# Block-sparse attention with a feed-forward layer: tying the first steps of the query and key preparations to the code's order

## The chip, the cores and the metric

The kernel runs on one core of a Trainium2 chip. The metric is the device time of one launch in microseconds (us). Two runs of the kernel before took 949.08 and 949.32 us, a median of 949.2 us.

The engines are named as the profile names them: PE multiplies matrices (PEld is its weight load), DVE and ACT work on vectors, POOL is a further vector engine, and SP issues the DMAs. In this kernel every DMA is issued by SP, in the order of its one instruction stream.

## The reference

For each of 4 batches and 8 heads there are 768 queries and 768 keys of 64 values, all in single precision. Attention is block-sparse with blocks of 32 tokens: a block of queries sees its own block and the two beside it, the first and the last block, and three sampled blocks (`sampled_blocks`, drawn with the inputs). The first and the last block of queries see all keys. Scores are divided by 8, masked, put through a softmax and multiplied with the values. The heads of a token are then laid side by side to 512 numbers, and a feed-forward layer follows:

```
h = x @ w_in                  # 3072 x 512 times 512 x 2048
g = maximum(0.01 * h, h)
out = g @ w_out               # 3072 x 2048 times 2048 x 512
```

## The kernel before, in words

**Precision.** Every operand of a matrix product is split into two half-precision parts, a high one and a low one, after a scaling by a power of two. To find that power of two for a piece of queries or keys, the kernel squares the piece and sums it.

**Tiling.** The work is cut into 192 units, one per batch, tile of 64 queries (two blocks) and pair of heads. Four tiles of queries are an *item*, so there are 12 items (three per batch, `b` and `j`). The outer loop (L1027) goes over the 192 units and is called a *step* each time. In one step it emits, in the order of the letters in `CFG["ord"]` (L45), pieces of many units in flight: scores on PE (`scores`, L629), mask and minimum on DVE (`unit_ttr`, L658), exponential on ACT (`unit_exp`, L669), the high part on ACT (`unit_high`, L684), the low part on DVE and a transposing DMA of the split probabilities `pp` into `pt` (`unit_split`, L689 and L692), the product with the values on PE (`pair_av`, L714), and pieces of the feed-forward layer of an earlier item (`ffn_h` L749, L756 to L766, `ffn_o` L779, `ffn_out` L797).

**Preparing queries.** `prep_q` (L518) makes one *half*: 128 queries of all heads, enough for two tiles, so 8 steps. There are 24 halves. Its chain is: the load of `rq` (L473, issued by `load_q`; there is one buffer of it), the square with its row sums on ACT (L523, the *first operation*), a product with a matrix of ones on PE that adds up the 128 partitions (L126, called from `scale_sum`, the *sum*), four small operations on DVE (L140 to L149), the high part on ACT (L530), the low part on DVE (L532), a transposing DMA (L535, `qs`) and two DMAs that swap the halves of the partitions (L537 and L538, `qxs`). The scores need `qs` and `qxs`. The function is a generator: `side_step` (L857), the letter "p" near the end of a step, advances such generators by a quota of work.

**Preparing keys.** `prep_k` (L485) does the same for a pair of heads with a square at L494, the sum at L126, L506, L508 and a transposing DMA at L512. There are 16 of them, 4 per batch. From the second batch on they share one buffer `k16`, and two buffers `rk` take the loads.

**What sets the order.** The code emits instructions in the order above, but this isn't the order in which they run. The framework's scheduler goes over the whole program with a priority for each instruction (its place in the code, mostly) and a model of how long each takes, and puts on each engine's stream whatever is ready first by that model. On the chip each engine then runs its stream in that fixed order, and an instruction whose input hasn't come holds up all behind it. An operation that reads only a loaded buffer, as the squares do, can so come to stand far ahead of its place in the code. Groups of matmuls that are emitted through `together` (L164) stay together.

Of the kernel before, what the change touches and what calls it, by code (L numbers as in the profile page):

```python
# [13 lines left out]
F32 = mybir.dt.float32  # L14
# [5 lines left out]
P = 128  # L20
# [9 lines left out]
CFG = {  # L30
    "ahead": 3,
    "av_lag": 3,
    "bs": 1500,
    "early": 2,
    "flag": 1,
    "g": 2,
    "g_at": 0,
    "ht": 1,
    "k_at": 6,
    "k_at0": 26,  # L40
# [10 lines left out]
    "rk": 2,  # L51
    "rmax": 1.0,
    "rmin": 0.0,
    "side": 1.2,
    "side0": 1.6,
    "spair": 1,
# [9 lines left out]
def tile_block_sparse_attention_ffn(  # L66
# [19 lines left out]
    nc = tc.nc  # L86
# [20 lines left out]
    pa = ctx.enter_context(tc.tile_pool(name="pa", bufs=2))  # L107
    pf = ctx.enter_context(tc.tile_pool(name="pf", bufs=2))
    dr = ctx.enter_context(tc.tile_pool(name="dr", bufs=2, space=bass.MemoryType.DRAM))
    ps_s = ctx.enter_context(tc.tile_pool(name="ps_s", bufs=2, space=bass.MemoryType.PSUM))  # L110
    ps_o = ctx.enter_context(tc.tile_pool(name="ps_o", bufs=2, space=bass.MemoryType.PSUM))
    ps_1 = ctx.enter_context(tc.tile_pool(name="ps_1", bufs=1, space=bass.MemoryType.PSUM))

# [1 line left out]
    nc.vector.memset(zero, 0.0)  # L115

    def bank(name, tag="h"):
        return ps_1.tile([P, 512], F32, tag=tag, name=name, bufs={"h": 3, "av": 1}[tag])


    ones = cst.tile([P, P], F32, name="ones")
# [2 lines left out]
    def scale_sum(ss, n, name):  # L124
        pb = bank(f"{name}_sum")
        nc.tensor.matmul(pb[:, :n], ones, ss, start=True, stop=True)  # L126
        return pb

    def scale_of(pb, n, name, total=False, keep=None, fl="q"):

        pool, tg = (sm, "sc") if keep is None else (cst, keep)
        m = 1 if total else n
        tot = sm.tile([P, 4], F32, tag=f"tot{fl}", name=f"{name}_tot")
        if total:
            nc.vector.tensor_reduce(out=tot[:, :1], in_=pb[:, :n], op=ALU.add, axis=AX.X)
            nc.vector.tensor_scalar(out=tot[:, :1], in0=tot[:, :1], scalar1=TINY, scalar2=None, op0=ALU.max)
        else:
            nc.vector.tensor_scalar(out=tot[:, :m], in0=pb[:, :m], scalar1=TINY, scalar2=None, op0=ALU.max)  # L140
        ex = sm.tile([P, 4], I32, tag=f"ex{fl}", name=f"{name}_ex")
        nc.vector.tensor_scalar(
            out=ex[:, :m], in0=tot[:, :m].bitcast(I32), scalar1=24, scalar2=23,
            op0=ALU.logical_shift_right, op1=ALU.logical_shift_left,
        )
        inv = pool.tile([P, 4], F32, tag=f"{tg}_i", name=f"{name}_inv")
        s = pool.tile([P, 4], F32, tag=f"{tg}_s", name=f"{name}_s")
        nc.vector.tensor_scalar(out=inv[:, :m], in0=ex[:, :m].bitcast(F32), scalar1=2.0 ** 50, scalar2=None, op0=ALU.mult)
        nc.vector.reciprocal(out=s[:, :m], in_=inv[:, :m])  # L149
        return inv, s  # L150
# [3 lines left out]
    def scales(ss, n, name, **how):  # L154
        now = tc.cur_priority
        tc.cur_priority = now - CFG["bs"]
        begin = len(nc.cur_bb.bb.instructions)
        pb = scale_sum(ss, n, name)
        loose.update(i.name for i in nc.cur_bb.bb.instructions[begin:])
        r = scale_of(pb, n, name, **how)  # L160
        tc.cur_priority = now + 8
        return r

    def together(emits):  # L164

        now = tc.cur_priority
        begin = len(nc.cur_bb.bb.instructions)
        for n, emit in enumerate(emits):
            if n == 1:
                tc.cur_priority = now - 100000  # L170
            emit()
        new = nc.cur_bb.bb.instructions[begin:]
        for i in new[1:]:
            tc.add_manual_dep(i, new[0].name, mybir.DependencyInfo(
                mybir.DependencyClass.NoSync, mybir.DependencyReason.DATA), reason="together")
        tc.cur_priority = now + len(new)
# [308 lines left out]
    def prep_k(b, hp, rk):  # L485

        nm = f"k{b}_{hp}"
        ss = sm.tile([P, 1], F32, tag="ssk", name=f"ss_{nm}")
        if b == 0:
            k16 = early_k.bitcast(F16)[:, (NP + hp) * 2 * S:(NP + hp + 1) * 2 * S].rearrange(  # L490
                "p (n l d) -> p n l d", n=HC, l=2)
        else:
            k16 = pa.tile([P, HC, 2, D], F16, tag="k16", name=f"k16_{nm}", bufs=1)
        nc.scalar.activation(flat(k16)[:, :S], flat(rk), AF.Square, accum_out=ss)  # L494
        yield 1.0
        yield 0.01
        pb = scale_sum(ss, 1, nm)
        yield 0.2
        inv, s = scale_of(pb, 1, nm, fl="k")
        if (b, "inv") not in kready:  # L500
            kready[b, "inv"] = cst.tile([P, NP], F32, name=f"kinv_{b}")
        nc.vector.tensor_scalar(
            out=kready[b, "inv"][:, hp:hp + 1], in0=inv[:, :1], scalar1=-SCALE, scalar2=None, op0=ALU.mult)
        yield 0.4
        raw = rk.rearrange("p h c d -> p (h c) d")
        nc.scalar.activation(k16[:, :, 1, :], raw, AF.Copy, scale=s[:, :1])  # L506
        yield 1.0
        nc.vector.scalar_tensor_tensor(  # L508
            out=k16[:, :, 0, :], in0=raw, scalar=s[:, :1], in1=k16[:, :, 1, :], op0=ALU.mult, op1=ALU.subtract)
        if b not in kts:  # L510
            kts[b] = pa.tile([P, H, S], F16, tag="kt", name=f"kt_{b}", bufs=2)
        nc.sync.dma_start_transpose(  # L512
            out=kts[b][:, 2 * hp:2 * hp + 2, :].rearrange("p h (c t) -> p (h c) t", t=P),
            in_=k16.rearrange("p n l d -> p (n l d)"))
        kready[b, hp] = True
        yield 1.2

    def prep_q(b, j, i, rq):  # L518

        nm = f"q{b}_{j}_{i}"  # L520
        ss = sm.tile([P, 1], F32, tag="ssq", name=f"ss_{nm}")
        qa = pa.tile([P, H, 2, D], F16, tag="qa", name=f"qa_{nm}", bufs=1)
        nc.scalar.activation(flat(qa)[:, :H * D], rq.rearrange("p h d -> p (h d)"), AF.Square, accum_out=ss)  # L523
        yield 0.7
        yield 0.01
        pb = scale_sum(ss, 1, nm)
        yield 0.2
        inv, s = scale_of(pb, 1, nm)
        yield 0.4
        nc.scalar.activation(qa[:, :, 1, :], rq, AF.Copy, scale=s[:, :1])  # L530
        yield 0.7
        nc.vector.scalar_tensor_tensor(  # L532
            out=qa[:, :, 0, :], in0=rq, scalar=s[:, :1], in1=qa[:, :, 1, :], op0=ALU.mult, op1=ALU.subtract)
        qs = pa.tile([P, H, P], F16, tag="qs", name=f"qs_{nm}", bufs=2)
        nc.sync.dma_start_transpose(out=qs, in_=flat(qa))  # L535
        qxs = pa.tile([P, H, P], F16, tag="qxs", name=f"qxs_{nm}", bufs=2)
        nc.sync.dma_start(out=qxs[:D], in_=qs[D:])  # L537
        nc.sync.dma_start(out=qxs[D:], in_=qs[:D])  # L538
        qstack[b, j, i] = (qs, qxs, inv)
        yield 0.8  # L540
# [157 lines left out]
    def pair_av(pr):  # L698

        if pr.hp == 0:  # L700
            avs[pr.item.n, pr.T] = bank(f"av_{pr.nm}", "av").rearrange("p (n l t) -> p n l t", n=NP, l=2)
        pr.av = avs[pr.item.n, pr.T]
        for u in pr.units:
            require_v(u.b, u.hp, u.T)
        emits = []
        for u in pr.units[::-1]:
            n = NCH * u.parts
            for c in range(n):
                for l in range(2):
                    for hh in range(2):  # L710
                        vt = vgs[u.b, u.T][:, c, 2 * u.hp + hh, :] if u.T else v16s[u.b, u.hp][:, c, hh, :]
                        emits.append(lambda o=pr.av[hh * D:(hh + 1) * D, u.hp], a=vt[:, l * D:(l + 1) * D],
                                     m=u.pt[c // NCH][:, :, c % NCH, hh * D:(hh + 1) * D], c=c, l=l, n=n:
                                     nc.tensor.matmul(o, a, m, start=(c == 0 and l == 0), stop=(c == n - 1 and l == 1)))  # L714
        together(emits)

    def tile_evac(pr):

# [93 lines left out]
    for b in range(B):  # L812
        for j in range(NI):
# [3 lines left out]
            for k_ in range(TPI):  # L817
                for hp in range(0, NP, 2):
                    pr = Unit()
# [30 lines left out]
    def require_v(b, hp, T):  # L850
        until(("v", b), lambda: (b, hp) in v16s if T == 0 else (b, "ready") in scr)
        while T and (b, T) not in vgs:
            start_gather_v()
# [76 lines left out]
    def start_q(n):  # L930
        if n < len(halves):
            start(("q", *halves[n]), prep_q(*halves[n], rq[n]))
# [8 lines left out]
    def start_k(b, hp):  # L941
        start(("k", b, hp), prep_k(b, hp, rk[b, hp]))
# [84 lines left out]
    for u in units:  # L1027
        it, ui = u.item, u.k * NP + u.hp
        b, nb = it.b, it.b + 1
# [161 lines left out]
```

## Time and profile before

| what | number |
|---|---|
| median of two runs | 949.2 us |
| the profiled execution, whole | 946.47 us |
| its span, first to last instruction | 944.7 us |
| PE busy | 754.8 us, 80% |
| DVE busy | 609.1 us, 64% |
| ACT busy | 488.1 us, 52% |
| POOL busy | 331.3 us, 35% |
| DMA queue, share of 16 engines | 68.5% |
| mean granted clock of PE | 0.931 |

The profile is one execution. Its span is 1.8 us shorter than its own time, and its time is 2.7 us under the median of the two runs. A row such as "L523 ACT ACTIVATE" is a group of instructions of line 523 on ACT. In a row of waits the engine on the left sat idle until what stands on the right was done; the three numbers are the total in us, how often, and the longest. SP's instructions aren't counted as busy time, so SP has no share in the table; its rows are marked "SPq" and are seen in the timeline and in the chain of waits.

### The profile page before, as it was taken

What the parts mean: (1) busy time and instruction counts of PE and PEld (TensorE: products, weight loads), DVE (VectorE), ACT (ScalarE), POOL (GpSimd) and SP (SyncE); (2) the same over time, 40 slices, a digit from 0 to 9 for tenths busy, and PEclk for the clock granted to TensorE, in tenths of its full rate; (3) what the DMA queues carried; (4) which work ended last, traced back from release to release, by engine and by line L of the source; (5) the groups of instructions that cost most, each with busy time, mean ns of one, the idle gap of its engine ahead of it and who ended that gap; (6) DMA issues with size and microseconds to landing.
All of it is one profiled execution on the core that took longest, in us unless ns stands there. A gap on an engine that the chain in (4) does not pass through costs nothing. (4 is left out here: it accounts for less than half of the span.)

```text
span 944.7 us, 21784 instructions
## 1 busy us (share of the span) xinstructions
PE 754.8 (80%) x7020; PEld 492.8 (52%) x7020; DVE 609.1 (64%) x1643; ACT 488.1 (52%) x1063; POOL 331.3 (35%) x469
## 2 busy tenths in 40 slices
PE   1325456788978979979897968989888988989998
PEld 1214334465645645646554635556455655656674
DVE  4989899996857667557565565567466655745221
ACT  4565768575535456456455554456355554535121
POOL 0234665542215344243324242333323433532221
PEclk9998557799989989999999998999999999989999
DMA  9996798678685767766675978676785665555200
GB/s 209 283 276 162 162 244 187 164 148 167 141 180 128 160 121 157 160 137 130 151 165 111 171 134 147 151 146 127 151 161 125 137 136 139 120 113 123 32 23 23
DMA packets 336624, 139.38 MB, mean 148 GB/s; under 512 B 299389, under 2 KB 311678, under 8 KB 336510
## 3 DMA queue, kind: packets, MB, share of 16 engines
q1 hardware_dynamic: 336510, 137.99, 68.5%
q8 instruction: 55, 0.90, 0.4%
q14 instruction: 59, 0.48, 0.2%
HBM read 65.57 MB, written 12.58 MB: 83 GB/s over the span
## 5 line engine op out<-in xcount | busy, mean ns | idle before, releaser
L779 PE MATMUL o<-W,g 128*128 128x512 f16 x1152 | 279.1, 388 | 7.6 <-ACT ob L797 2.9
L749 PE MATMUL h<-x,W 128*128 128x256 f16 x2304 | 280.9, 279 | 0.3 <-DVE ht L760 0.3
L749 PEld LDWEIGHTS <-W 128*128 128x128 f16 x2304 | 227.2, 101 | 50.7 <-issue 10.5
L766 POOL TENSOR_TENSOR g<-ht,g 128x512 f16<-128x512 f32 x96 | 115.3, 1201 | 336.5 <-DVE g L765 201.2
L689 DVE SCALAR_TENSOR_TENSOR pp<-p,r,pp 128x384 f16<-128x384 f32 x208 | 142.5, 702 | 106.0 <-ACT pp L684 104.4
L779 PEld LDWEIGHTS <-g 128*128 128x128 f16 x1152 | 108.8, 100 | 137.4 <-issue 23.9
L669 ACT ACTIVATE p<-p,mx 128x384 f32<-128x384 f32 x208 | 125.8, 606 | 96.3 <-DVE mx L658 67.0
L591 POOL COPY kg<-kt 128x256 f16 x264 | 129.3, 510 | 131.6 <-PE s L651 74.9
L684 ACT ACTIVATE pp<-p,r 128x384 f16<-128x384 f32 x208 | 119.6, 607 | 103.9 <-DMA pt<-pp 72.0
L714 PE MATMUL av<-pt,vg 128*64 128x128 f16 x2112 | 83.0, 231 | 50.5 <-DMA pt<-pp 40.3
L658 DVE CUSTOM_DVE_ANT_0 p<-s,em,nsc 128x384 f32<-128x384 f32 x176 | 101.9, 609 | 21.1 <-PE s L651 20.0
L714 PEld LDWEIGHTS <-vg 128*64 128x64 f16 x2112 | 72.1, 116 | 77.0 <-issue 57.4
L760 DVE SCALAR_TENSOR_TENSOR ht<-h,gd,ht 128x512 f32<-128x512 f32 x80 | 59.8, 747 | 56.0 <-ACT ht L756 55.7
L756 ACT ACTIVATE ht<-h,gs 128x512 f32<-128x512 f32 x80 | 54.0, 675 | 63.9 <-PE h L749 48.7
L651 PE MATMUL s<-kg,qs_q 128*64 128x384 f16 x352 | 65.1, 364 | 12.1 <-DVE mx L658 7.7
L732 POOL TENSOR_TENSOR x<-xf,x 128x256 f16<-128x256 f32 x48 | 35.8, 745 | 90.7 <-ACT x L730 90.0
L651 PE MATMUL s<-kg,qxs_q 128*64 128x384 f16 x352 | 63.9, 357 | 4.3 <-DMA qxs_q<-qs_q 4.3
L651 PEld LDWEIGHTS <-qs_q 128*64 128x64 f16 x416 | 27.9, 116 | 68.7 <-issue 45.4
L523 ACT ACTIVATE qa_q<-rq 128x512 f16<-128x512 f32 x25 | 15.7, 628 | 68.9 <-DMA rq<-in_q_dram 68.9
L765 DVE CAST g<-ht 128x512 f16<-128x512 f32 x96 | 43.4, 452 | 8.9 <-PE o L779 7.5
L677 DVE TENSOR_SCALAR sum<-sum 128x2 f32<-128x2 f32 x96 | 24.9, 259 | 37.1 <-ACT p L669 36.1
L669 ACT ACTIVATION_READ_ACCUMULATOR p<-p,mx 128x1 f32 x208 | 38.9, 187 | 0.0
(126 smaller groups left out, 726.0 us busy)
## 6 DMA issues: line engine op xcount, KB each, us to landing
vg<-scr SPq DMA_DIRECT2D x280, 64.0 KB, 1.9
vg<-scr SPq DMA_DIRECT2D x44, 256.0 KB, 3.1
v<-in_v_dram SPq DMA_DIRECT2D x32, 192.0 KB, 3.4
qxs_q<-qs_q SPq DMA_DIRECT2D x48, 128.0 KB, 3.0
scr<-v SPq DMA_DIRECT2D x16, 384.0 KB, 3.7
W<-in_moe_w_in_dram SPq DMA_DIRECT2D x5, 1024.0 KB, 5.9
rq<-in_q_dram SPq DMA_DIRECT2D x20, 256.0 KB, 3.5
out_dram<-ob SPq DMA_DIRECT2D x20, 256.0 KB, 2.3
```

The costliest lines, as they stand in the source:

```text
L591: nc.gpsimd.tensor_copy(out=kg[:, :, slot * BLOCK:(slot + 1) * BLOCK], in_=kt[:, :, bass.ds(off, BLOCK)])
L651: nc.tensor.matmul(o, a, k, start=(n == 0), stop=(n == 1)))
L658: nc.vector.tensor_tensor_reduce(out=u.p[i], in0=u.sp[i], in1=kgs[u.b, u.T][1] if u.T else zero.to_broadcast([P, KEYS]), scale=u.nsc, scal ...
L669: nc.scalar.activation(u.p[i], u.p[i], AF.Exp, scale=-1.0, bias=u.mx[:, :1], accum_out=u.pair.sum[:, u.pi, i:i + 1])
L684: nc.scalar.activation(pp[:, 0, :], p, AF.Copy, scale=u.r)
L689: nc.vector.scalar_tensor_tensor(out=pp[:, 1, :], in0=p, scalar=u.r, in1=pp[:, 0, :], op0=ALU.mult, op1=ALU.subtract)
L714: nc.tensor.matmul(o, a, m, start=(c == 0 and l == 0), stop=(c == n - 1 and l == 1)))
L749: nc.tensor.matmul(c.ph[:, i], w, x, start=(d == 0 and m == 0), stop=(d == NP - 1 and m == 2)))
L756: nc.scalar.activation(c.t, c.ph, AF.Copy, scale=scale[1])
L760: nc.vector.scalar_tensor_tensor(out=c.t, in0=c.ph, scalar=scale[0], in1=c.t, op0=ALU.mult, op1=ALU.max)
L766: nc.gpsimd.tensor_tensor(out=c.g[:, 1], in0=c.t, in1=c.g[:, 0], op=ALU.subtract)
L779: nc.tensor.matmul(o, a, w, start=(c.first and i == 0 and m == 0), stop=(c.last and i == 1 and m == 2)))
```

## The change

A new function `hold` finds, in the code's order, the last instruction emitted before a given one on the same engine, and ties the given one behind it. The tie is an order for the scheduler, without a semaphore; no instruction is added to the stream. It is applied to the first operation (ACT) and to the sum (PE) of each preparation of queries and of keys, except in the first item of the first batch for queries and in the whole first batch for keys: 22 preparations of queries and 12 of keys. The diff also names two numbers of buffers through a setting "s" with the value 2, which leaves them at 2 and 3 as before, and adds a tie for the products with the values that the setting "hold" with its value "kq" leaves off.

```diff
+    "hold": "kq",
+    "s": 2,
...
-    ps_s = ctx.enter_context(tc.tile_pool(name="ps_s", bufs=2, space=bass.MemoryType.PSUM))
+    ps_s = ctx.enter_context(tc.tile_pool(name="ps_s", bufs=CFG["s"], space=bass.MemoryType.PSUM))
...
-        return ps_1.tile([P, 512], F32, tag=tag, name=name, bufs={"h": 3, "av": 1}[tag])
+        return ps_1.tile([P, 512], F32, tag=tag, name=name, bufs={"h": 5 - CFG["s"], "av": 1}[tag])
...
+    def hold(begin):
+
+        ins = nc.cur_bb.bb.instructions
+        prev = next((i for i in reversed(ins[:begin]) if i.engine == ins[begin].engine), None)
+        if prev is not None:
+            tc.add_manual_dep(ins[begin], prev.name, mybir.DependencyInfo(
+                mybir.DependencyClass.NoSync, mybir.DependencyReason.DATA), reason="hold")
+
+    count = lambda: len(nc.cur_bb.bb.instructions)
...
+        begin = count()
         nc.scalar.activation(flat(k16)[:, :S], flat(rk), AF.Square, accum_out=ss)
+        if b and "k" in CFG["hold"]:
+            hold(begin)
         yield 1.0
         yield 0.01
+        begin = count()
         pb = scale_sum(ss, 1, nm)
+        if b and "k" in CFG["hold"]:
+            hold(begin)
...
+        later = (b or j) and "q" in CFG["hold"]
+        begin = count()
         nc.scalar.activation(flat(qa)[:, :H * D], rq.rearrange("p h d -> p (h d)"), AF.Square, accum_out=ss)
+        if later:
+            hold(begin)
         yield 0.7
         yield 0.01
+        begin = count()
         pb = scale_sum(ss, 1, nm)
+        if later:
+            hold(begin)
...
+        begin = count()
         together(emits)
+        if pr.item.n and "a" in CFG["hold"]:
+            hold(begin)
```

## The prediction

> **What bounds the kernel now.** I began with the page, to see whether one engine fills the span.
>
> ```profile
> span 944.7 us, 21784 instructions
> PE 754.8 (80%) x7020; PEld 492.8 (52%) x7020; DVE 609.1 (64%) x1643; ACT 488.1 (52%) x1063; POOL 331.3 (35%) x469
> PE 22%; DMA 5%; SPq 2%; DVE 1%; ACT 1%; issue 1%; ACTq 0%
> PE o L779 9%; PE h L749 9%; DMA pt<-pp 3%; PE av L714 2%; PE s L651 2%; DMA qs_q<-qa_q 1%; DMA rq<-in_q_dram 1%; SPq L619 1%; SPq L621 1%; DVE p L658 0%; DVE pp L689 0%; ACT p L669 0%; ACT pp L684 0%; DMA qxs_q<-qs_q 0%; DVE ht L760 0%
> ```
>
> PE is the busiest engine, and it still idles for 944.7 - 754.8 = 190 us. ACT is busy for half of the span. The share of a whole span says little, so the second view was the busy time by stage. Its columns give the stretch, its length, the five engines, the granted clock, the DMA share and GB/s.
>
> ```profile
> 0.00:250.00 250.00, 142.48 (x1291) 95.19 (x1293) 211.51 (x560) 155.02 (x302) 100.75 (x115) 0.84 0.87 196
> 250.00:850.00 600.00, 521.44 (x5009) 337.95 (x5004) 369.90 (x1025) 308.48 (x714) 209.59 (x335) 0.96 0.69 143
> 850.00:945.00 95.00, 90.87 (x729) 59.66 (x727) 27.74 (x59) 24.56 (x47) 20.96 (x20) 0.99 0.23 50
> ```
>
> There are three stages. Up to 250 us the weights are split, and DVE leads with 211.5 of 250 us. From 250 to 850 us attention and feed-forward run together: PE has 600 - 521.4 = 78.6 us of idle time there, and ACT and DVE have far more. After 850 us PE runs almost alone. What the change can win lies mostly in the 78.6 us.
>
> Third, the waits of the engines that the change touches, ACT's rows first.
>
> ```profile
> ACT pp L684 <- DMA pt<-pp: 72.0, 33, 6.8
> ACT qa_q L523 <- DMA rq<-in_q_dram: 68.9, 20, 6.3
> ACT k_k L494 <- DMA kt<-k_k: 26.0, 7, 8.5
> ...
> PE av L714 <- DMA pt<-pp: 54.7, 29, 5.3
> PE k_sum L126 <- ACT k_k L494: 20.8, 7, 4.9
> PE s L651 <- DMA qs_q<-qa_q: 12.5, 4, 9.6
> PE q_sum L126 <- ACT qa_q L523: 2.9, 2, 2.7
> ```
>
> The square of the queries (L523) holds ACT idle for 68.9 us in 20 waits for its load, 3.4 us each. This is what the change takes hold of. But PE waits for the sums of queries only 2.9 us. Its largest wait is for `pt`, the transposed probabilities, and ACT's largest wait is for the same DMA: there are six buffers `pp`, and ACT gets none until SP has sent an old one off. An engine that waits for its output to be carried away is ahead of its carrier. So the fourth view was the carrier: SP's timeline, and the chain of waits through one of PE's longer pauses.
>
> ```profile
> 489.05 0.52 SPq L611 DMA_DIRECT2D vg<-scr  x1
> 489.62 1.54 SPq L616 DMA_DIRECT2D vg<-scr  x2
> 491.27 1.21 SPq L692 DMA_TRANSPOSE pt<-pp  x1
> 492.58 1.25 SPq L535 DMA_TRANSPOSE qs_q<-qa_q  x1
> 493.89 0.57 SPq L473 DMA_DIRECT2D rq<-in_q_dram  x1
> 494.56 1.29 SPq L692 DMA_TRANSPOSE pt<-pp  x1
> ```
>
> ```profile
> 756.96 1.22 SPq L692
> ...
> 765.84 0.06 issue
> 765.95 2.78 DMA pt<-pp
> 768.77 0.94 PE av L714 x24
> ```
>
> ```profile
> SPq L808 <- ACT ob L797: 60.7, 4, 40.4
> SPq L692 <- DVE pp L689: 13.3, 13, 1.4
> ```
>
> SP's rows follow one another with about 0.1 us between them. Before PE's pause that ends at 768.77 us the chain runs through SP instructions for 9 us without a wait. The only large wait of SP, 60.7 us, is for the outputs in the tail. So up to its last transposition SP issues without a stop, and its stream is the bound of attention. The Trainium skill has this case in "Perfetto Trace Analysis", section "What DMA-bound means": the issuing engine's track is solid with DMA slices. By that rule a wait on ACT that goes away leaves the time at 949. The trace agrees, by the rows just shown.
>
> The fifth view is the tail: SP's last transpositions, PE's last product with values, and PE's last work.
>
> ```profile
> 874.94 4.63 SPq L692 DMA_TRANSPOSE pt<-pp  x3
> 895.63 0.86 PE L714 MATMUL av<-pt,vg 128*64 128x128 f16 x24
> 934.66 6.21 PE L779 MATMUL o<-W,g 128*128 128x512 f16 x28
> ```
>
> SP ends at 874.94 + 4.63 = 879.6 us. With 2.8 us for landing (the row above) the last product could start at 882.4; it starts at 895.6, as PE is still busy with older feed-forward work. What follows it, about 45 us, is the last item's feed-forward part, which needs all of its tiles. So PE's backlog is worth at most 895.6 - 882.4 = 13 us as long as SP ends where it does.
>
> **The change part by part.** No instruction is added: the ties are orders within one engine. What moves is seen best in one preparation (ACT, PE and DVE rows; SP's are above at 492.58 and 493.89).
>
> ```profile
> 465.41 0.63 ACT L523 ACTIVATE qa_q<-rq 128x512 f16<-128x512 f32 x1 [6.25 <-DMA rq<-in_q_dram]
> ...
> 470.77 0.67 ACT L756 ACTIVATE ht<-h,gs 128x512 f32<-128x512 f32 x1
> ...
> 484.61 0.38 PE L126 MATMUL q_sum<-ss_q,ones 128*128 128x1 f32 x2
> ...
> 488.67 0.75 DVE L532 SCALAR_TENSOR_TENSOR qa_q<-rq,q_s,qa_q 128x512 f16<-128x512 f32 x1
> ```
>
> *The squares of queries* (22 held). ACT waits 6.25 us for a load here, then squares. In the code's order the square stands behind the activation `ht` at 470.77, so it would start at 471.44, 6.0 us later, and the wait is gone. The sum runs only at 484.61, nearly 19 us after the square, so nothing behind it moves: not the low part at 488.67, not the transposition that SP reaches at 492.58, 3.2 us after that has ended (489.42), nor the two swaps and the next load of `rq`, which needs its one buffer back from L532. For the square alone the price is zero, covered by those 19 us.
>
> What does ACT's idle time give when it goes? The upper bound is 68.9 us; the lower one is 0, as ACT then waits for `pp` buffers instead. Between them, the page's chain puts about 1% of the span, some 9 us, on the load `rq`, and the next late thing in that chain is SP. I take less than half of it, 4 us, because a pause of PE that ends with an SP transfer only grows by what an earlier pause loses.
>
> *The squares of keys* (12 held). Their 26.0 us on ACT are waits for `kt<-k_k`, the single buffer `k16` being carried away by SP, not for loads. Put beside the code's order, most of these squares run behind their neighbour already, so the tie does nothing, and both this wait and PE's 20.8 us on their sums stay. Bounds: 0 to 20.8 us; I take 0.
>
> *The sums.* In the preparation above the sum already follows its preceding group in the code, so its tie does nothing. It does where the sum had jumped ahead:
>
> ```profile
> 291.13 0.63 ACT L523 ACTIVATE qa_q<-rq 128x512 f16<-128x512 f32 x1 [4.59 <-DMA rq<-in_q_dram]
> 298.70 0.38 PE L126 MATMUL q_sum<-ss_q,ones 128*128 128x1 f32 x2
> 308.24 1.17 DVE L532 SCALAR_TENSOR_TENSOR qa_q<-rq,q_s,qa_q 128x512 f16<-128x512 f32 x1
> 309.98 0.61 ACT L669 ACTIVATE p<-p,mx 128x384 f32<-128x384 f32 x1 [1.87 <-DVE mx L658]
> 317.03 1.67 SPq L535 DMA_TRANSPOSE qs_q<-qa_q  x1
> 321.59 0.60 SPq L538 DMA_DIRECT2D qxs_q<-qs_q  x1
> 331.15 0.35 PE L651 MATMUL s<-kg,qs_q 128*64 128x384 f16 x2 [0.57 <-DVE mx L658]
> ```
>
> Here the code places the square behind the activation at 309.98, so it starts at 310.6 and ends with its read-out near 311.4. The sum follows at 311.4 instead of 298.7, 12.7 us later, and the low part ends at 308.24 + 1.17 + 12.7 = 322.1. SP stands ready for the transposition at 317.03. If the plan leaves it there, SP waits 5.1 us, and the queue behind it with it: the load of the next queries, the swaps, the transpositions of `pp` and the gathers of values. With 2.8 us for landing, as for the transposition at 765.95, the swap is there near 321.6 + 0.6 + 2.8 + 5.1 = 330.1, still before the scores at 331.15. This is the dearest preparation of the later stage that I found by placing each held operation behind its code neighbour; most cost nothing. The scheduler also plans anew and can move the transposition back. Bounds of the cost: 0 to 22 x 5.1 = 112 us; I take 1 us, nearest to the preparation with 19 us in hand.
>
> *The first stage.* Squares of the first batch's second item would move most, since ACT's stream there is full of weight work. PE has 250 - 142.5 = 107 us free there and DVE doesn't wait for queries, so I take 0, with 10 us of either sign in the range.
>
> The sum: 946.47 - 4 + 1 = 943.5 us for the profiled execution. The median of the runs lies 2.7 us higher, so the forecast is 946 us. A new plan for 21784 instructions also shuffles neighbours without a cause that I can name; I allow the tail's 13 us each way for that.
>
> **The rivals.**
>
> *ACT's stalls do reach PE.* PE then saves time in the middle stage until the last product follows SP at 882.4, and the time is 946.47 - 13 + 2.7 = 936 us. For it: the chain names the load `rq`, and PE's 78.6 idle us would hold it. Against it: ACT waits 72.0 us for `pp` buffers. If SP also ended sooner, all 68.9 us could come back, 946.47 - 68.9 + 2.7 = 880 us, which the solid rows of SP speak against. The Trainium skill would lead there: "DMA: Bandwidth & Descriptors", section "Rules for kernel authors", tells authors to issue a DMA early and to wait late, so that its fixed cost overlaps, and the tie is just such a later wait.
>
> *SP is held up by late preparations (slower).* The mechanism is the 5.1 us wait at L535. With SP without a pause, each such wait moves its end. From four of the 22 preparations it costs 20 us, over 2%; with six it costs 31 us and gives 946.47 + 31 + 2.7 = 980 us. For it: four waits of PE for `qs` (12.5 us) show that some queries come just in time now. Against it: the preparation at 465 us doesn't move beyond its square.
>
> *The tie does nothing.* Where the scheduler had each operation behind its neighbour already, the order stays, and so does 949 us. For the sums and keys this is partly so; the squares of queries with 20 waits speak against it for the whole.
>
> **How the numbers follow.** A measurement of this kernel can tell about 2%, so 930 to 968 us counts as no change. Chances: the forecast 0.63, between 936 and 956 us; ACT's stalls reaching PE 0.18, of which 0.04 for 880 us and 0.08 more below 930 us once the shuffle helps; held up 0.10, of which 0.08 over 968 us; nothing happens 0.09. So faster has 0.12, no change 0.80, slower 0.08. The range reaches to 932 us, just under the tail's bound, and to 962 us, the forecast with the shuffle's 13 us and 3 us of late preparations; it leaves out about 0.1 at each end.
>
> **What would show it.** In the changed kernel's waits, L523 on `rq` should fall from 68.9 us to under 25, and the squares should stand behind the exponentials or `ht`. SP's last transposition should still start between 870 and 885 us, with rows that touch up to there, and ACT's wait for `pt<-pp` should stay or grow. PE's busy time from 250 to 850 us should stay within some 10 us of 521. I'm wrong if SP's last transposition comes before 865 us, or if PE's last product with values follows SP within 5 us; wrong the other way if SP shows waits at L535 that add up to 20 us.

## The result and the profile after

The changed kernel takes 959.07 us (two runs, 958.65 and 959.48), the kernel before 949.2 us: a ratio of 1.011, with a 95% interval of 1.0083 to 1.0136. It is 1% slower. That is inside the 2% that count as no change, and on the other side of 949 us than the forecast of 946. It lies inside the range of 932 to 962 us, but outside the 936 to 956 us that had the chance of 0.63: the range reaches it only by the 13 us that were allowed for a shuffle without a cause. The profiled execution took 958.65 us against 946.47.

The page of the changed kernel, its span and busy times:

```profile
span 956.9 us, 21796 instructions
PE 760.0 (79%) x7020; PEld 495.1 (52%) x7020; DVE 617.9 (65%) x1643; ACT 489.5 (51%) x1063; POOL 323.1 (34%) x469
```

The span has grown by 956.9 - 944.7 = 12.2 us, with the same 7020 matmuls. The three stages of the prediction, in the changed kernel (stretch, length, PE, PEld, DVE, ACT, POOL, granted clock, DMA share, GB/s):

```profile
0.00:250.00 250.00, 132.89 (x1216) 90.83 (x1218) 201.98 (x530) 149.48 (x293) 88.51 (x112) 0.85 0.83 189
250.00:850.00 600.00, 527.44 (x5010) 338.57 (x5005) 384.04 (x1044) 312.18 (x716) 212.36 (x337) 0.95 0.69 143
850.00:957.00 107.00, 99.70 (x804) 65.67 (x801) 31.85 (x70) 27.88 (x55) 22.27 (x21) 0.98 0.26 59
```

In the first 250 us PE does 75 matmuls fewer than before (1216 against 1291), DVE 9.5 us less and POOL 12 us less. The middle stage does as much as before, and the tail takes over what is left. So the loss is in the first stage. Two stretches of it, first before, then after the change:

```profile
50.00:100.00 50.00, 20.15 (x216) 14.67 (x217) 43.76 (x104) 30.88 (x58) 18.94 (x19) 0.87 0.84 206
100.00:150.00 50.00, 25.51 (x256) 17.22 (x253) 45.95 (x96) 36.45 (x71) 35.32 (x38) 0.53 0.91 203
```

```profile
50.00:100.00 50.00, 20.64 (x208) 14.13 (x209) 41.27 (x87) 25.24 (x51) 15.65 (x20) 0.94 0.78 211
100.00:150.00 50.00, 19.82 (x208) 15.01 (x202) 38.99 (x92) 33.97 (x60) 24.16 (x27) 0.60 0.84 195
```

DVE, which leads there, loses 2.5 and 7.0 us, ACT 5.6 and 2.5 us, in a hundred microseconds. POOL and PE lose most in the second of these stretches, in which all of them do less. SP's transpositions of `pp`, counted in their order, give the same picture as a pace:

| transposition | starts before | starts after | later by |
|---|---|---|---|
| 9th | 94.6 | 90.9 | -3.7 |
| 17th | 115.5 | 126.9 | 11.4 |
| 25th | 148.9 | 162.3 | 13.4 |
| 33rd | 187.6 | 194.7 | 7.1 |
| 65th | 322.3 | 335.5 | 13.2 |
| 208th, the last | 877.6 | 892.2 | 14.6 |

The delay arises between the 9th and the 25th. It is half as long at the 33rd, is back at the 65th, and stays for over 500 us. The tail repeats it. SP's last rows and two of PE's in the changed kernel:

```profile
888.31 5.09 SPq L717 DMA_TRANSPOSE pt<-pp  x3
```

```profile
907.83 0.86 PE L739 MATMUL av<-pt,vg 128*64 128x128 f16 x24
945.13 7.93 PE L807 MATMUL o<-W,g 128*128 128x512 f16 x36
```

SP ends at 893.4 us (879.6 before), PE's last product with values starts 14.4 us after that (16.1 before), and the feed-forward part follows.

The waits of the changed kernel that answer to the rows of the prediction:

```profile
ACT pp L709 <- DMA pt<-pp: 121.0, 58, 6.6
PE av L739 <- DMA pt<-pp: 55.2, 25, 8.1
PE s L676 <- DMA qs_q<-qa_q: 20.0, 7, 9.6
PE s L676 <- DMA qxs_q<-qs_q: 17.4, 11, 2.7
ACT k_k L507 <- DMA kt<-k_k: 16.9, 7, 7.6
PE k_sum L128 <- ACT k_k L507: 14.8, 5, 4.8
```

The 68.9 us that ACT waited for `rq` have no row left: the ties did what they say. Instead ACT waits 49 us longer for buffers of `pp` (72.0 before). PE's waits for queries have grown from 12.5 us to 20.0, and from 7.8 to 17.4 for the swapped ones.

What happens between the 9th and the 25th transposition is seen in one half, the first of the first batch's second item. Its rows before (ACT's square and high part and the next decoding of weights, SP's transposition and the four of `pp` behind it):

```profile
58.34 0.62 ACT L523 ACTIVATE qa_q<-rq 128x512 f16<-128x512 f32 x1
...
72.30 0.72 ACT L530 ACTIVATE qa_q<-rq,q_s 128x512 f16<-128x512 f32 x1 [3.82 <-DVE q_s L149]
...
107.62 1.13 ACT L310 ACTIVATE W<-W 128x1024 f32<-128x1024 f32 x1 [1.05 <-DMA W<-in_moe_w_in_dram]
```

```profile
90.73 1.27 SPq L535 DMA_TRANSPOSE qs_q<-qa_q  x1
...
94.57 5.28 SPq L692 DMA_TRANSPOSE pt<-pp  x4
```

And after, ACT's rows, DVE's and SP's:

```profile
87.00 0.61 ACT L543 ACTIVATE qa_q<-rq 128x512 f16<-128x512 f32 x1
...
103.71 1.12 ACT L322 ACTIVATE W<-W 128x1024 f32<-128x1024 f32 x1 [9.85 <-DMA W<-in_moe_w_in_dram]
104.72 0.71 ACT L555 ACTIVATE qa_q<-rq,q_s 128x512 f16<-128x512 f32 x1
```

```profile
94.47 0.15 DVE L151 RECIPROCAL q_s<-q_inv 128x1 f32<-128x1 f32 x1
...
104.86 0.69 DVE L323 TENSOR_SCALAR W<-W 128x1024 f32<-128x1024 f32 x1 [5.98 <-ACT W L322]
```

```profile
96.17 1.83 SPq L316 DMA_DIRECT2D W<-in_moe_w_in_dram  x2
98.12 9.54 SPq L717 DMA_TRANSPOSE pt<-pp  x4
...
110.44 3.85 SPq L560 DMA_TRANSPOSE qs_q<-qa_q  x1
```

The square runs 28.7 us later (87.0 against 58.3). Its scale is there at 94.6, but ACT's stream now has the decoding of a piece of weights (L322; L310 in the kernel before, where it stands behind the high part) ahead of the high part, and that piece's load is issued only at 96.17. ACT stands 9.85 us for it, with the high part and the exponentials behind it; DVE stands 5.98 us for ACT. The high part runs 32.4 us later than before, the transposition 19.7 us later, and the half's first scores start at 118.2 instead of 110.4. In the new plan ACT waits for a load that was issued too late for the decoding's new place.

That is what ACT and DVE lost. SP lost its time another way, and the whole delay of 13 us is SP's. From the 9th to the 25th transposition of `pp` SP took 71.4 us (54.4 before), and in both kernels its pauses between rows add up to under 1 us there. So SP didn't stand and wait for the late half: its low part had ended at 106.42, 4 us before SP came to its transposition. SP's stream had grown. The 16 transpositions of `pp` took 28.4 us instead of 20.9, two of queries 5.1 us where one took 1.3, and four loads of `v` (2.6 us) had moved in from later. The four transpositions that took 5.28 us before take 9.54 us, as they stand behind two loads of weights issued one right after the other. The second and the third of the four:

```profile
100.17 3.54 SPq L717 DMA_TRANSPOSE pt<-pp  x1
103.81 2.51 SPq L717 DMA_TRANSPOSE pt<-pp  x1
```

The first of these ends at 103.71 us, when ACT's wait for the first load ends too. The second ends at 106.32, and the second load lands at 106.39. Up to its last transposition SP issues the same 785 DMAs in both kernels and pauses as long (19.7 us before, 20.3 after), but the rows of these DMAs add up to 614.4 us instead of 599.3.

### The profile page after: what moved, and what is told of

It is laid out like the page before. It is cut to its first block, busy times and chain, and to the rows that moved or that the text cites. A ratio compares the mean times of both kernels' runs of the same rounds, so it can differ in the third digit from the quotient of the medians.

```text
span 956.9 us, 21796 instructions
## 1 busy us (share of the span) xinstructions
PE 760.0 (79%) x7020; PEld 495.1 (52%) x7020; DVE 617.9 (65%) x1643; ACT 489.5 (51%) x1063; POOL 323.1 (34%) x469
## 5 line engine op out<-in xcount | busy, mean ns | idle before, releaser
L616 POOL COPY kg<-kt 128x256 f16 x264 | 121.0, 477 | 144.5 <-PE s L676 81.2
L784 ACT ACTIVATE ht<-h,gs 128x512 f32<-128x512 f32 x80 | 54.0, 675 | 68.9 <-PE h L777 57.5
L702 DVE TENSOR_SCALAR sum<-sum 128x2 f32<-128x2 f32 x96 | 25.3, 264 | 23.1 <-ACT p L694 22.5
L676 PEld LDWEIGHTS <-qxs_q 128*64 128x64 f16 x416 | 26.1, 118 | 25.3 <-DMA qxs_q<-qs_q 20.4
```

The source lines that it names most:

```text
L616: nc.gpsimd.tensor_copy(out=kg[:, :, slot * BLOCK:(slot + 1) * BLOCK], in_=kt[:, :, bass.ds(off, BLOCK)])
L676: nc.tensor.matmul(o, a, k, start=(n == 0), stop=(n == 1)))
L784: nc.scalar.activation(c.t, c.ph, AF.Copy, scale=scale[1])
```

## The experiments

Eighteen runs. The kernel before took 943.8 to 945.1 us (medians) on the chips of the experiments, some 5 us less than in the comparison above, so all are judged by their ratio to it.

| run | what is tied or moved | ratio | 95% interval |
|---|---|---|---|
| e1_later_only | ties from the second batch on | 1.0022 | 0.9995 to 1.0049 |
| e2_first_only | the ties that e1 leaves out | 1.010 | 1.0057 to 1.0144 |
| e3_one_half | one half only | 1.0111 | 1.0062 to 1.016 |
| e4_squares_only | all squares, no sums | 1.0147 | 1.0102 to 1.0192 |
| e8_more_sp | no tie, 100 more DMAs on SP | 1.0516 | 1.0463 to 1.057 |
| e9_short_tie | that half's square, tied less far back | 0.9996 | 0.9972 to 1.002 |
| e10_half_tie | the same, half the way | 1.0058 | 1.0033 to 1.0083 |
| e11_gathers_pool | no tie, all sampled gathers on POOL | 1.0467 | 1.0413 to 1.052 |
| e12_relief_act | no tie, loads of `v` and stores on ACT | 0.9983 | 0.9958 to 1.0009 |
| e12_relief_pool | no tie, the same on POOL | 1.006 | 1.003 to 1.0089 |
| e13_relief_ties_act | e12_relief_act and e1's ties | 0.9894 | 0.9844 to 0.9944 |
| e14_one_pool | no tie, one gather in six on POOL | 0.9867 | 0.9812 to 0.9922 |
| e15_pool_later | e14 and e1's ties | 0.999 | 0.9965 to 1.0015 |
| e16_pool_all | e14 and all ties of the change | 0.9932 | 0.9903 to 0.9962 |
| e17_all_but_half | all ties but the one half's | 1.0113 | 1.0061 to 1.0164 |
| e18_both_later | e12_relief_act, e14 and e1's ties | 0.9856 | 0.9825 to 0.9887 |
| e19_all_but_half_again | e17 once more | 1.0082 | 1.005 to 1.0114 |
| e20_other_three | the first batch's other three halves only | 1.0036 | 1.0012 to 1.006 |

### Which ties cost: the first batch against the rest

The first theory was that the first batch's ties cost the time, the rival that it comes from all ties a little, or from the sums. e1 ties only what is emitted from the second batch's work on (the keys of the second batch are prepared in the first, hence `b > 1`); e2 is its complement.

```diff
-        if b and "k" in CFG["hold"]:
+        if b > 1 and "k" in CFG["hold"]:
...
-        later = (b or j) and "q" in CFG["hold"]
+        later = b and "q" in CFG["hold"]
```

> Ties only on preparations emitted from the second batch on (queries of batches 1 to 3, keys of batches 2 and 3); those of the first batch run untied as before. First-stage theory: the 10 us were lost with the late queries of the first batch, and the later ties are free, so 946 to 951 us. Rival, late sums: the later ties each cost a little, so 955 us or more. Rival, shuffle: any new order gives some number between 940 and 960 us, with no link to the stage.

```diff
-        if b and "k" in CFG["hold"]:
+        if b == 1 and "k" in CFG["hold"]:
...
-        later = (b or j) and "q" in CFG["hold"]
+        later = b == 0 and j and "q" in CFG["hold"]
```

> The complement: ties only on preparations emitted in the first batch (queries of its second and third item, keys of batch 1). First-stage theory: 955 to 961 us, and the middle stage as long as before. Late sums: 948 to 952 us. Shuffle: no link.

e3 ties one half, the one shown above, and no keys; e4 takes the ties of the sums away.

```diff
-        if b and "k" in CFG["hold"]:
+        if False:
...
-        later = (b or j) and "q" in CFG["hold"]
+        later = (b, j, i) == (0, 1, 0)
```

> One preparation alone is tied, the first half of the first batch's second item, whose square moved from 58 to 87 us and whose first scores moved from 110 to 118 us. If this half is the cause: 953 to 960 us, with SP some 10 us behind from 130 us on. If the loss is spread over the first batch's ties: 948 to 952 us.

```diff
         pb = scale_sum(ss, 1, nm)
-        if b and "k" in CFG["hold"]:
-            hold(begin)
...
         pb = scale_sum(ss, 1, nm)
-        if later:
-            hold(begin)
```

> Squares tied, sums left free. First-stage theory: the square itself is what comes 30 us later in the first batch, and its sum can't run before it, so 954 to 960 us. Late sums: the ties of the sums are gone, so 946 to 951 us, with ACT's wait of L543 for rq still near 0.

Measured: 1.0022 for the later ties, 1.010 for the first batch's, 1.0111 for one half alone, 1.0147 with the sums free. The 18 later halves and 8 later keys cost nothing that is seen, the tie of one half's square and sum reproduces the size of the loss, and the sums' ties are not what costs. ACT's rows of e3 show the same stall as the changed kernel's:

```profile
85.70 0.61 ACT L543 ACTIVATE qa_q<-rq 128x512 f16<-128x512 f32 x1
...
100.64 1.12 ACT L322 ACTIVATE W<-W 128x1024 f32<-128x1024 f32 x1 [8.34 <-DMA W<-in_moe_w_in_dram]
101.66 0.71 ACT L555 ACTIVATE qa_q<-rq,q_s 128x512 f16<-128x512 f32 x1
```

In e2 the wait is 6.61 us, in e4 6.70 us. In e1 two decodings between 100 and 125 us wait 1.07 and 1.03 us, about as before (1.05 and 1.29).

SP's rows go the same way. With the change, e2, e3 and e4 the 16 transpositions of `pp` from the 9th to the 25th take 27.6 to 28.8 us (20.9 before), and the 25th starts 9 to 13 us late; in e1 they take 20.4 us, and it starts 2 us early. In e2, e3 and e4 too, two of the long transpositions end within 0.1 us of the landing of a load of weights just ahead of them. So these four kernels, which tie this half's square behind the last activation, share three things: the late half, ACT's stall, and the long rows on SP. One tie brings all three, and none of the four separates them, so which of them the time follows is not isolated. Only the rows on SP account for SP's delay there. Long rows don't always cost in the end: e14 and e15 have them too (27.3 and 27.9 us), with fewer gathers left on SP.

### How late may that square be?

If lateness is what costs, a shorter delay should cost less. e9 and e10 tie the same square alone, without its sum, behind an activation that stands 26 or 21 places back instead of the last.

```diff
-    def hold(begin):
+    def hold(begin, back=1):
...
-        prev = next((i for i in reversed(ins[:begin]) if i.engine == ins[begin].engine), None)
+        prev = [i for i in ins[:begin] if i.engine == ins[begin].engine and isinstance(i, mybir.InstActivation)][-back]
...
-        later = (b or j) and "q" in CFG["hold"]
+        later = (b, j, i) == (0, 1, 0)
...
         if later:
-            hold(begin)
+            hold(begin, 26)
```

> Only the square of the one half of the first batch is tied, and behind an activation that ran at 67 us instead of the one at 92 us: some 9 us later than before instead of 29 us. If any lateness there costs in proportion: 3 us, ratio 1.003. If the first 10 us are free: ratio 0.998 to 1.002.

> The same square tied behind an activation that ran at 75 us: some 16 us later than before. In proportion: 5 to 6 us, ratio 1.006. If there is a point from which it decides, when the chain of some 40 us no longer ends before the scores at 110 us: 0 to 5 us, ratio 1.000 to 1.005. If the tie's cost comes from the new order as such and not from lateness: 10 us as with the full tie.

ACT's square and high part of this half, in e9 and then in e10:

```profile
66.36 0.61 ACT L543 ACTIVATE qa_q<-rq 128x512 f16<-128x512 f32 x1
...
73.49 0.71 ACT L553 ACTIVATE qa_q<-rq,q_s 128x512 f16<-128x512 f32 x1
```

```profile
73.12 0.61 ACT L543 ACTIVATE qa_q<-rq 128x512 f16<-128x512 f32 x1
...
83.14 0.72 ACT L553 ACTIVATE qa_q<-rq,q_s 128x512 f16<-128x512 f32 x1 [0.23 <-DVE q_s L151]
```

The square at 66.4 us costs nothing (0.9996): its high part runs only 1.2 us later than before. At 73.1, with the high part 10.8 us later, it costs 0.6%; at 85.7 (e3), with the high part 29.4 us later, 1.1%. In order of time this looks like a price of lateness, but e10's trace doesn't bear it out. The first scores of its half start at 108.3 us, sooner than before (110.4), SP's 25th transposition at 148.7 (148.9) and the 97th at 462.9 (462.4). What is lost is lost after that: the last starts at 882.6 (877.6). So in this trace e10's loss doesn't come from the half being late, but from the rest of the new plan, far from the tie. That is the shuffle of e1's expectation, and a part of some tenths of a per cent isn't excluded in the other runs either.

### Do the other ties cost too?

If the one half were the whole loss, all ties but its own should be free.

```diff
-        later = (b or j) and "q" in CFG["hold"]
+        later = (b or j) and (b, j, i) != (0, 1, 0) and "q" in CFG["hold"]
```

> The changed kernel with every tie but those of one half, the first half of the second item of the first batch. If that half is the whole loss: 0.998 to 1.004 of the kernel before. If the other ties of the first batch cost as well: 1.005 to 1.010.

It measured 1.0113, against that reading. It was run again, beside a kernel that ties only the three other halves of the first batch.

> The changed kernel with every tie but those of the first half of the second item of the first batch, the same kernel as the run that measured 1.0113 (1.0061 to 1.0164), in more rounds. If the other three tied halves of the first batch cost as much as that one half does alone: 1.008 to 1.015 of the kernel before. If that run was one of a spread of a few microseconds: 1.001 to 1.006.

```diff
-        if b and "k" in CFG["hold"]:
+        if False:
...
-        later = (b or j) and "q" in CFG["hold"]
+        later = (b, j, i) in ((0, 1, 1), (0, 2, 0), (0, 2, 1))
```

> Only the three other halves of the first batch are tied (the second half of the second item, both halves of the third), nothing else. If they cost by themselves: 1.005 to 1.012 of the kernel before, with the first scores of those halves later than before and the transpositions of the probabilities behind before's from there on. If the first half of the second item is the whole loss: 0.998 to 1.003.

The three halves alone cost 0.4%, a little more than was expected of nothing; all ties but one half's cost 0.8%, which is e20's 0.4% and e1's 0.2% within their intervals. But e19 also ties the keys of the second batch, which neither of the two does, and these keys have no run of their own. The one half's 1.1% and these 0.8% don't add up to the change's 1.1%, so the costs overlap. The one half is enough for the whole loss, but it isn't needed for one.

In e19 the loss has another form. SP's rows add up to 599.2 us, as before, but its pauses to 25.3 us instead of 19.7. From 165 to 250 us they are 9.5 us, and 8.3 in e17's trace of the same kernel, against 4.2 before and 6.2 in e20. Of these traces only e17's and e19's have a longer pause (3.8 and 3.1 us) ahead of a transposition of `pp`, in e19 between these rows:

```profile
200.43 5.35 SPq L646 DMA_DIRECT2D vg<-scr  x6
210.10 3.14 SPq L717 DMA_TRANSPOSE pt<-pp  x2
```

The first scores of the third item's first half start at 200.8 us there (198.9 in e17), against 187.0 before and 187.5 in e20, which ties the same half. That points to the ties of the keys, and no run shows it.

### Does SP pace the rest?

The prediction rests on SP's stream being the bound, so that ACT's waits are worth nothing. If so, 100 more short instructions on SP must cost their own issue time.

```diff
+        if 64 <= step < 164:
+            junk = sm.tile([NB, 8], F32, tag="junk", name=f"junk_{step}", bufs=4)
+            nc.sync.dma_start(out=junk, in_=c_iota[:, :8])
```

> The kernel before with one more DMA of 32 bytes a row for SP to issue in each of the steps 64 to 163, 100 in all, that nobody waits for. If SP's issue paces the middle stage, each costs its issue of some 0.4 to 0.6 us in the time: 35 to 60 us, so a ratio of 1.04 to 1.065. If SP only looks busy and ACT, DVE or PE set the pace: under 10 us, ratio under 1.01.

The added DMAs in its trace (shortest, median and longest in ns), and ACT's wait there:

```profile
L1056 SPq DMA_DIRECT2D junk<-in_iota_dram x100: 305/540/2667, 58.8 to 821.6; - x100
```

```profile
ACT pp L684 <- DMA pt<-pp: 129.4, 67, 7.5
```

A ratio of 1.0516 on 944.0 us is 48.7 us more for 100 DMAs, 0.49 us each, near the median of 0.54 us that SP spends on one. SP's issue time comes out one for one, and ACT's wait for `pp` grows from 72.0 to 129.4 us.

### Relieving SP, and the ties again

Then the ties should pay as soon as SP has less to do. e12 moves the loads of `v` and the stores to another engine's queue, e13 adds e1's ties.

```diff
-            nc.sync.dma_start(out=t[:, :, h, :], in_=v[b, 2 * hp + h].rearrange("(c p) d -> p c d", p=P))
+            nc.scalar.dma_start(out=t[:, :, h, :], in_=v[b, 2 * hp + h].rearrange("(c p) d -> p c d", p=P))
...
-                nc.sync.dma_start(out=out[r0:r0 + P, :], in_=ob)
+                nc.scalar.dma_start(out=out[r0:r0 + P, :], in_=ob)
```

> The kernel before with the loads of values and the stores of the outputs, 60 issues that take 34 us of SP's stream, issued by ACT. If SP paces attention, SP's last transposition comes some 30 us earlier and the time falls until PE is the bound: 915 to 935 us on a chip where before takes 945 (ratio 0.97 to 0.99). If something else paces: 0.995 or more.

> The same 60 issues on POOL instead of ACT. If it is SP's stream that counts and not which engine takes the work: the same as the relief by ACT within 1%. If POOL's own order gets in the way, as with the 264 gathers on POOL: above the kernel before.

> The same relief of SP with the ties of the second batch on (as in the run with the later ties only). If ACT's wait for the queries' load was only hidden behind SP, the ties pay now: 0.5 to 1% under the relief alone. If SP still paces: the same as the relief alone within 0.3%.

ACT's waits in e12_relief_act, then in e13:

```profile
ACT qa_q L523 <- DMA rq<-in_q_dram: 49.5, 20, 4.9
ACT pp L684 <- DMA pt<-pp: 48.6, 30, 4.8
```

```profile
ACT pp L709 <- DMA pt<-pp: 82.2, 35, 5.2
ACT qa_q L543 <- DMA rq<-in_q_dram: 4.9, 3, 2.8
```

The move by itself gives nothing on ACT (0.9983) and costs 0.6% on POOL. For ACT, that is what was expected if something else than SP set the pace. SP has 34 us less to issue, but its last transposition ends only 2.2 us sooner (877.4 against 879.6), and its pauses grow from 19.7 to 52.5 us. So another engine is close behind SP: what is added to SP costs in full, what is taken off it doesn't come back in full. With the ties on top it is 0.9894, 0.9% below, and SP's last transposition ends at 869.1 us. The ties do pay here.

The sampled gathers are the larger part of SP's stream. e11 moves all 264 of them to POOL, e14 one of the six of each tile.

```diff
-            off = nc.sync.value_load(offs[:1, i:i + 1], min_val=0, max_val=S - BLOCK)
+            off = nc.gpsimd.value_load(offs[:1, i:i + 1], min_val=0, max_val=S - BLOCK)
...
-            nc.sync.dma_start(out=vg[ps, c, :], in_=scr[b][bass.ds(off, BLOCK), :])
+            nc.gpsimd.dma_start(out=vg[ps, c, :], in_=scr[b][bass.ds(off, BLOCK), :])
```

> The kernel before with the 264 sampled gathers of values issued by POOL instead of SP, which takes some 290 us of 880 off SP's stream. If SP paces the kernel: PE or POOL takes over and the time falls by 3% or more, to between 850 and 920 us. If not: within 1% of the kernel before, or slower as POOL is held up.

```diff
-            off = nc.sync.value_load(offs[:1, i:i + 1], min_val=0, max_val=S - BLOCK)
+            eng, q_ = (nc.gpsimd, "vp") if slot in (6,) else (nc.sync, "v")
+            off = eng.value_load(offs[:1, i:i + 1], min_val=0, max_val=S - BLOCK)
...
-            nc.sync.dma_start(out=vg[ps, c, :], in_=scr[b][bass.ds(off, BLOCK), :])
-            in_order("v", begin)
+            eng.dma_start(out=vg[ps, c, :], in_=scr[b][bass.ds(off, BLOCK), :])
+            in_order(q_, begin)
```

> One of the six sampled gathers of each tile on POOL, 44 issues or some 48 us off SP. If SP paces: ratio 0.96 to 0.99, and the loss with all 264 was POOL's load. If any DMA from POOL delays its other work: above 1.0.

All gathers on POOL lose 4.7%: POOL's busy time goes from 331 to 461.5 us, and SP pauses for over 300 us. One in six gains 1.3%, the best of the runs with no tie: SP's last transposition ends at 859.4 us, 20 us sooner than before. Then the ties on top of that:

> The kernel before with the sixth sampled gather of each tile issued by GpSimd (which alone measured 0.987 of the kernel before), and the ties of the change from the second batch on. If the ties save ACT's waits for rq as soon as SP has less to issue: 0.5 to 1% below that, 0.975 to 0.983 of the kernel before, and no row of waits for rq. If the ties give nothing here either, because another engine bounds by now: 0.985 to 0.990.

> The same gathers on GpSimd, with all ties of the change, those of the first batch too. If the first batch's tied half costs its 10 us whatever SP has to issue: about 1% above the run that ties from the second batch on, 0.985 to 0.995 of the kernel before. If SP, lightened, makes that up: within 0.3% of that run.

> The sixth gather of each tile on GpSimd, the loads of v and the stores of the output on ACT's queue, and the ties from the second batch on. If SP still paces: below the run with the gather and the ties alone, 0.965 to 0.980 of the kernel before. If PE or ACT bounds by now: the same as that run, or above it.

The waits for queries in e14, then in e15:

```profile
ACT qa_q L523 <- DMA rq<-in_q_dram: 77.4, 20, 6.5
PE s L652 <- DMA qs_q<-qa_q: 18.2, 6, 8.4
PE s L652 <- DMA qxs_q<-qs_q: 12.1, 7, 2.9
```

```profile
ACT qa_q L543 <- DMA rq<-in_q_dram: 18.0, 4, 6.7
PE s L677 <- DMA qs_q<-qa_q: 23.4, 8, 9.0
PE s L677 <- DMA qxs_q<-qs_q: 22.1, 11, 3.2
```

Here the ties cost 1.2% (0.999 against 0.9867, on two chips, each beside the kernel before), though ACT's wait for `rq` falls from 77.4 to 18.0 us: PE now waits 45.5 us for queries instead of 30.3, and the last half's first scores start at 833.4 instead of 823.7 us. That they must pay once SP is relieved has fallen. With all ties of the change the time is 0.9932, under the later ties' 0.999, so the first batch's loss doesn't carry over either. Its number lies in the range of e16's first expectation, but neither 1% above e15, as that one had it, nor within 0.3% of it. Both reliefs with the ties (e18) give 0.9856, the same as e14's 0.9867 within the intervals. In sum the ties on the same 18 halves measured +0.2%, -0.9% and +1.2%, depending on what else is in the plan. PE's waits for `qs` and `qxs` together went from 20.3 to 27.6 us in the first case (e1), from 31.8 to 33.0 in the second (e13), and from 30.3 to 45.5 in the third: the ties take away ACT's waits every time, and cost where they take the queries' lead with them. That is a reading of three pairs, and no run isolates it.

e14 beats both kernels with less change than e18, at 929.8 us against 943.9.

## Why the prediction was wrong

*SP's issue stream bounds attention*: right, in one direction. 100 added DMAs cost 0.49 us each (e8), and the later ties change nothing (1.0022, e1) while ACT's waits move from the loads to `pp`. Taking 60 DMAs off SP gave 0.2% on ACT's queue, which isn't clear of nothing (0.9958 to 1.0009, e12), so another bound lies close behind. The rule of the Trainium skill in "Perfetto Trace Analysis", section "What DMA-bound means", leads to 949 us, if SP's stream takes as long as before. For the later ties the runs agree with it. For the whole change they don't: SP's rows take 15.1 us more (614.4 against 599.3).

*The squares of queries, a gain of 4 us*: mis-sized, it is 0 (e1). The reason that I gave against a gain was the stronger one. The wait for `rq` fell to under 25 us and ACT's wait for `pt<-pp` grew, as said.

*The price of zero for the moved square, covered by 19 us*: it was read from one half of the middle stage and carried over to all. The halves of the later batches bear it out (e1). In the first batch a square 8.0 us later was free (e9), and one 27.4 us later cost 1.1% (e3).

*The first stage*: this is the step that failed. "I take 0, with 10 us of either sign" measured +12.2 us in the profiled execution, and e2 gives the first batch 1.0% alone. The step saw that these squares "would move most, since ACT's stream there is full of weight work", and then priced them by PE's 107 us of idle time. That idle time was not cover: PE waits there for what this chain delivers, 4.3 us for this half's `qs` alone, where it waited for none before. DVE, which led the stage, "doesn't wait for queries" but waits for ACT (5.98 us), whose decoding with a late load (9.85 us) stood ahead of the high part. And SP, which the prediction took for the bound of attention alone, is solid in this stage too: under 1 us of pauses from the 9th to the 25th transposition. So whatever lengthens SP's stream there delays what follows, and with the loads of weights and values moved together it took 17.0 us more for this stretch. The prediction put the new order of SP's stream in this stage at nothing. That SP's rows are longer is measured; that the loads make them so is read from where these rows end, and no run varies the loads alone.

*The sums, 1 us*: nothing more is seen; without their ties the loss stays (1.0147, e4). *The squares of keys, 0*: their wait fell from 26.0 to 16.9 us and PE's on their sums from 20.8 to 14.8, and nothing came of it.

*SP held up by late preparations*: the rival of the right sign, with the wrong mechanism. The list of SP's waits has 26.3 us at these transpositions, over my threshold of 20, but 21.4 in the kernel before already: I had set a threshold without the value before. Nor are they waits: the largest, 3.9 us, is put down to an operation on the weights and is the whole row at 110.44, though the low part that this row carries off was ready 4 us before. The pauses between SP's rows ahead of these transpositions add up to 2.1 us before and 1.6 after. SP's rows grew, and SP didn't stand. *ACT's stalls reach PE*: refuted for this kernel by e1. *The tie does nothing*: refuted by the waits.

*What would show it*: SP's last transposition started at 892.2, outside my 870 to 885, 14.6 us later than before, most of which SP lost in the first stage. PE's busy time from 250 to 850 us is 527.44, within 10 us of 521. PE's last product with values follows SP by 14.4 us, so the tail's 13 us were never touched. The tail moved with SP, as said.

## What to carry to other kernels

A tie on one engine makes a new plan for all of them. Before pricing it at zero, ask in each stage how much lead the consumers of the moved operation have, what is queued next to its new place on the same engine, above all an instruction whose load is issued late, and what the new plan does to the stream that sets the pace. Idle time of an engine is cover only if it isn't waiting for the chain that is delayed. And where one engine's issue stream paces a stage, the gain lies in what that stream carries: here one gather in six, given to another queue, won 1.3%, where taking away ACT's waits for `rq` (68.9 us before, 9.5 with the later ties) won nothing. Not every relief pays: 60 loads and stores moved off SP won nothing that is clear of noise.

## What the hardware showed that was not expected

A small DMA on a solid issue stream isn't hidden: 100 DMAs of 24 rows of 32 bytes cost 48.7 us, though the queue kept the 16 DMA engines busy for only 68.5% of the span before.

Which engine issues a DMA matters, and its idle time doesn't tell how. The loads of `v` and the stores give 0.9983 on ACT and 1.006 on POOL; 44 gathers on POOL give 0.9867 and 264 give 1.0467, with POOL busy for 35% of the span before. The Trainium skill, in "Perfetto Trace Analysis", section "DMA Optimizations", says that balancing DMAs over the engines that can issue them may help where issuing is the bottleneck. These runs agree for a part of the gathers and not for all of them.

A transposing DMA of `pp` takes SP 1.25 us in the median of 208 and up to 3.60 us; the one of the queries took 1.27 us before (at 90.73) and 3.85 us after (at 110.44), right behind a load of weights and three of values. A row is longer here while larger loads issued just ahead of it are still on their way: two transpositions in each of four kernels (the changed one, e2, e3, e4) end within 0.1 us of the landing of a load of weights. Behind a single load of weights (101.94 before) the two transpositions took 1.24 and 1.39 us. No run varies the loads alone, so this is a reading of rows.
